# Two row gathers in place of one, four filler matmuls, and other cuts of two early loads

## The chip, the cores and the metric

The kernel runs on one core of a Trainium2 chip. Time is device microseconds (us) of one launch, the median of several runs. The core has a matrix engine (PE, whose loading of weights the profile lists as PEld), a vector engine (DVE), a scalar engine (ACT), a general engine (POOL) and a queue engine (SP). Loads and stores are issued from SP's, ACT's and POOL's queues and carried out by 16 DMA engines.

## The reference

```
xn = layernorm(x)                                   # x: 8 x 1 x 512
q  = (xn @ wq) as 32 heads of 128                   # wq: 512 x 4096
k, v = the last 2048 rows of 8192 of each of 8 heads, each shared by 4 query heads
p  = softmax(q . k * 128 ** -0.5)
s  = (p . v) @ wo                                   # wo: 4096 x 512
h  = sigmoid(xn @ w_gate) * (xn @ w_up)             # 512 x 1792 each
g  = silu(h @ w_down)                               # w_down: 1792 x 512
out = x + s * g                                     # 8 batches, bfloat16
```

Only the window of the caches is read: 2 MB of k and of v for each half of a batch's heads, 32 loads of 2 MB in all, beside some 13.6 MB of weights.

## The kernel before, in words

**The ring.** All large inputs pass through `ring`, nine slots of 16 KB in each of 128 partitions. A list `todo` holds the loads in order: w_gate (two loads of two rows of each partition), w_up, the last 1152 rows of w_down (`want_down`), the slot for the other 640 rows (`want_side`, cleared by DVE), wq (two slots), 17 drains of SP's queue, then k and v in turns with k three ahead, then wo in pieces of 16, 10, 4 and 2 rows. `pump` issues as long as slots are free; `free` gives slots back after the code that last reads them, so SP's queue waits at a load until PE has used up an older one. All but the gather go through SP's queue. The input x is loaded in five pieces from ACT's queue (L200).

**The gather.** The first 640 rows of w_down are 64 pieces of ten rows (10 KB). One indirect DMA on POOL's queue (L239) puts each into a partition of its own; `SEGS` (L139, L140) says into which: (start, count, step). The other 64 partitions are given an index beyond the bound and stay cleared. The index is made on the chip: `sel` (copies of columns of the identity, on POOL) times `ranks` on PE, turned into `which` on DVE. Which partition holds a piece decides which DMA engine writes it.

**Early work.** Layer norm of x (L256 to L267), its transposes (L278), w_gate (L323) and w_up (L339) matmuls, h, its 19 transposes (L358: nine for the direct rows, ten for the gathered), q (L387), a `spot` matmul that spreads the gathered part of h to the partitions in use (L398), 19 matmuls with w_down (L403), the transposes of q.

**The batch loop** (L675). For each of eight batches: transposes of k on PE (L484), copied by DVE (L489), scores (L502), maximum and exponentials (L515, L522), transposes of p (L591), and the products with v (L612) two batches behind. After the loop the last batches are finished: scores, `row_max`, `values`, `combine`, `normalise`, `turn`. Between these stand fillers, `keep(n)`: n matmuls of 480 columns into `idle_ps`, which nobody reads (L720). The product with wo (L372, `fin_ps`, 128 matmuls in two halves of 64), two DVE operations and two stores end the kernel.

Of the kernel before, what the change touches and what calls it, by code (L numbers as in the profile page):

```python
# [10 lines left out]
def kernel(  # L11
# [13 lines left out]
    nc = tc.nc  # L25
# [90 lines left out]
    def want_rows(name, w, per, r0, r1, steps):  # L116
        n = -(-(r1 - r0) * w.shape[1] // (CT * Dh))

        def f(k):
            t, where = room(k, n, r1 - r0, w.shape[1])  # L120
            a = r0
            for step in steps:
                q0.dma_start(
                    out=t[:, a - r0 : a - r0 + step, :].rearrange("p r n -> p (r n)"),
                    in_=w.rearrange("(p r) n -> p r n", r=per)[
                        :, a : a + step, :
                    ].rearrange("p r n -> p (r n)"),
                )
                a += step
            rows_of[(name, r0)] = (t, where)  # L130
            for r in range(r0, r1):
                weights[(name, r)] = t[:, r - r0, :]

        todo.append((n, f))

    MT = 9
    SF = 10
    NSEL = 64
    SEGS = [(0, 15, 1), (16, 3, 1), (28, 18, 1), (48, 2, 1)]  # L139
    SEGS += [(60, 8, 1), (68, 6, 4), (92, 8, 1), (124, 4, 1)]  # L140
    m0 = NSEL * SF
    assert sum(n for _, n, _ in SEGS) == NSEL and m0 + MT * P == F
    side = {}

    def want_side(w):
# [35 lines left out]

    RT = 32
    Z = 32
    want_rows("wg_sb", B_w_gate, KT, 0, KT, (2, 2))
    want_rows("wu_sb", B_w_up, KT, 0, KT, (KT,))
    want_down(B_w_down)
    want_side(B_w_down)
    want_rows("wq_sb", A_wq, KT, 0, KT, (KT,))
    todo.append((0, lambda k: [q0.drain() for _ in range(17)]))
    order = [(b, i) for b in range(B) for i in range(NQ)]  # L190
    AHEAD = 3
    for n in range(len(order) + AHEAD):
# [4 lines left out]
    want_rows("wo_sb", A_wo, RT, 0, RT, (16, 10, 4, 2))  # L197

    x_bf = work.tile([B, D], bf16, name="x_bf")
    for r, z in ((0, 2), (2, 4), (4, 6), (6, 7), (7, 8)):  # L200
        q1.dma_start(out=x_bf[r:z], in_=A_x.flatten_outer_dims()[r:z])

    eps_t = work.tile([B, 1], f32, name="eps_t")
# [4 lines left out]
    make_identity(nc, ident_f[:])  # L208
    pump()

    sel = consts.tile([NSEL, P], bf16, name="sel")
    nc.gpsimd.memzero(sel[:])
    at = 0
    for p, n, step in SEGS:
        nc.gpsimd.tensor_copy(
            out=sel[:, p : p + (n - 1) * step + 1 : step],
            in_=ident[:NSEL, at : at + n],
        )
        at += n
    ranks = consts.tile([NSEL, 1], bf16, name="ranks")  # L220
    nc.gpsimd.iota(
        ranks[:],
        pattern=[[0, 1]],
        base=P,
        channel_multiplier=-1,
        allow_small_or_imprecise_dtypes=True,
    )
    rank_ps = ps_m.tile([P, 1], f32, name="rank_ps", tag="m")
    nc.tensor.matmul(rank_ps[:], lhsT=sel[:], rhs=ranks[:], start=True, stop=True)
    which = consts.tile([P, 1], mybir.dt.uint32, name="which")  # L230
    nc.vector.tensor_scalar(
        out=which[:],
        in0=rank_ps[:],
        scalar1=-1.0,
        scalar2=float(P),
        op0=ALU.mult,
        op1=ALU.add,
    )
    nc.gpsimd.indirect_dma_start(  # L239
        out=side["t"].rearrange("p t n -> p (t n)"),  # L240
        out_offset=None,
        in_=B_w_down[:m0, :].rearrange("(p t) n -> p (t n)", t=SF),
        in_offset=bass.IndirectOffsetOnAxis(ap=which[:, :1], axis=0),
        bounds_check=NSEL - 1,
        oob_is_err=False,
    )

    perm = consts.tile([P, P], bf16, name="perm")
    nc.gpsimd.tensor_copy(
# [102 lines left out]
    free(rows_of[("wu_sb", 0)])  # L352
    hT_ps = ps_m.tile([P, MT + SF, B], bf16, name="hT_ps", tag="m")
    cuts = [h_bf[:B, m0:F].rearrange("b (p t) -> b t p", t=MT)[:, t] for t in range(MT)]
    cuts += [h_bf[:B, :m0].rearrange("b (p t) -> b t p", t=SF)[:, t] for t in range(SF)]
    rows = [P] * MT + [NSEL] * SF
    for t, x in enumerate(cuts):
        nc.tensor.transpose(  # L358
            out=hT_ps[: rows[t], t, :], in_=x, identity=ident[:B, :B]
        )  # L360
    nc.vector.tensor_copy(out=hT_sb[:, :MT, :B], in_=hT_ps[:, :MT])
    hc_sb = work.tile([NSEL, SF, B], bf16, name="hc_sb")
    nc.scalar.copy(out=hc_sb[:], in_=hT_ps[:NSEL, MT:])

    NG = NB // 2
    ZO = Z * NG
# [28 lines left out]
                )  # L395
    free(rows_of[("wq_sb", 0)])
    spot_ps = ps_t.tile([P, SF, B], f32, name="spot_ps", tag="t")
    nc.tensor.matmul(spot_ps[:], lhsT=sel[:], rhs=hc_sb[:], start=True, stop=True)  # L398
    nc.scalar.copy(out=hT_sb[:, MT:, :B], in_=spot_ps[:])
    d_ps = ps_s.tile([P, D], f32, name="d_ps", tag="s")  # L400
    for t in range(MT + SF):
# [93 lines left out]
    def scores(b, u):  # L495
        i, j = u // NJ, u % NJ
        if u == 0:
            s_ps[b] = ps_s.tile([P, CU * PG], f32, name="s_ps", tag="s")
        t = kT.pop((b, u))
        o = M0 - rep * u  # L500
        for l in range(G):
            nc.tensor.matmul(  # L502
                s_ps[b][NR * l : NR * (l + 1), :],
                lhsT=qm_sb[:, b, i * G + l, o : o + Z],
                rhs=t[:, :, PG * l : PG * (l + 1)],
                start=(u == 0),
                stop=(u == NU - 1),
                tile_position=(0, NR * l),
                skip_group_check=True,
            )  # L510


    def row_max(b):
        st[b] = small.tile([P, 1], f32, name="st")
        nc.vector.tensor_reduce(  # L515
            out=st[b][:], in_=s_ps[b][:], axis=AX.X, op=ALU.max, negate=True
        )
        sums = small.tile([P, 1], f32, name="sums")
        s = s_ps.pop(b)
        for l in range(G):  # L520
            rows = slice(NR * l, NR * (l + 1))
            nc.scalar.activation(  # L522
                out=p_buf[b % 2][rows, :, l, :],
                in_=s[rows, :].rearrange("k (c p) -> k p c", p=PG),
                func=AF.Exp,
                bias=st[b][rows, :],
                accum_out=sums[rows, :],
            )
        fac[b] = sums
# [56 lines left out]
    def p_transposes(b, h):  # L586
        if h == 0:
            pT[b] = ppool.tile([P, CU, P], bf16, name="pT_sb")
        pT_ps = ps_t.tile([P, CH, P], bf16, name="pT_ps", tag="t")
        for c in range(CH):  # L590
            nc.tensor.transpose(  # L591
                out=pT_ps[:, c, :],
                in_=p_buf[b % 2][:, :, :, h * CH + c].rearrange("k p l -> k (p l)"),
                identity=turn_rows[:],
            )
        nc.vector.tensor_copy(out=pT[b][:, h * CH : (h + 1) * CH, :], in_=pT_ps[:])  # L596
# [27 lines left out]
    def values(b, c):  # L624
        for i in range(NQ):
            value(b, i, c)

    def combine(b):
        del pT[b]
        n = NJ if b < WIDE else 2  # L630
        o = small.tile([P, NJ, Dh], f32, name="o_sb")
        nc.scalar.activation(  # L632
            out=o[:, :n], in_=o_ps[:, :n], func=AF.Copy, scale=fac.pop(b)[:]
        )
        row[b] = o

    def normalise(b, oT_ps=oT_ps):
        o = row.pop(b)
        sel = sel_j if b < WIDE else sel_e
        n = NJ if b < WIDE else 2  # L640
        for e in range(n):
            nc.tensor.matmul(  # L642
                oT_ps,
                lhsT=o[:, e, :],
                rhs=sel[:, e],
                start=(e == 0),
                stop=(e == n - 1),
            )

        oB = small.tile([P, Hq, NDQ], bf16, name="oB")  # L650
        nc.vector.tensor_tensor(
            out=oB[:],
            in0=oT_ps.unsqueeze(2).to_broadcast([P, Hq, NDQ]),
            in1=band[:].unsqueeze(1).to_broadcast([P, Hq, NDQ]),
            op=ALU.mult,
        )
        row[b] = oB

    def turn(b, oP_ps=oP_ps):
        nc.tensor.matmul(  # L660
            oP_ps,
            lhsT=row.pop(b)[:].rearrange("p s q -> p (s q)"),
            rhs=pick[:],
            start=True,
            stop=True,
        )
        nc.vector.tensor_copy(out=oP_sb[:, :, 2 + 2 * b], in_=oP_ps)
# [3 lines left out]
    def values_some(b, u):  # L671
        for c in range(CV * u, CV * (u + 1)):
            values(b, c)
# [24 lines left out]
                f()  # L698

    last = B - 1  # L700
    scores(last, NU - 1)
    values_some(last - 2, NU - 1)
    combine(last - 2)
    row_max(last)
    values(last - 1, 0)
    values(last - 1, 1)
    normalise(last - 2)
    for c in range(2, CU):
        values(last - 1, c)
        if c == 5:  # L710
            turn(last - 2)
    combine(last - 1)
    stat_rows(last)
    p_transposes(last, 0)
    idle_ps = ps_s.tile([P, 512], f32, name="idle_ps", tag="s")
    idle_in = qm_sb[:, 0].rearrange("k h m -> k (h m)")

    def keep(n):
        for _ in range(n):
            nc.tensor.matmul(  # L720
                idle_ps[:, : Hkv * (M0 + Z)],
                lhsT=ident[:],
                rhs=idle_in,
                start=True,
                stop=True,
            )

    keep(2)
    for c in range(CU // 2):
        value(last, 0, c)  # L730
# [65 lines left out]
```

## Time and profile before

| | us |
|---|---|
| median of 3 runs (lowest to highest) | 198.5 (198.39 to 198.58) |
| the profiled execution, its own time | 198.86 |
| its span on the core | 197.1 |
| PE busy, share of the span | 163.4 (83%) |
| DVE | 125.7 (64%) |
| ACT | 40.8 (21%) |
| POOL | 9.1 (5%) |

The span is the time from the first to the last instruction of the core; the rest of the execution's time lies around it. Busy times of engines overlap. A row of a timeline gives start, busy time, engine, line, operation, output and inputs, and in brackets the idle time before it with what ended it. A row of a chain gives start, duration and what the end had to wait for. A row of stretches gives the stretch, its length, busy time of each engine (with instructions), the clock granted to PE as a share of its full speed, the share of the 16 DMA engines in use, and GB/s.

### The profile page before, as it was taken

The numbers are of one execution on the slowest core, as the hardware profiler recorded it, in microseconds if no ns is written. First come the engines' busy times: TensorE is split into PE (matmuls) and PEld (weight loads), VectorE is DVE, ScalarE is ACT, GpSimd is POOL, SyncE is SP. The second block draws the span as 40 slices with busy tenths as digits, with TensorE's granted clock in tenths as the row PEclk, the third lists the DMA queues.
The fourth block names the chain that finished last, engine by engine and source line by source line (L and its number), as shares of the span: only waits on it lengthen the run. The fifth ranks groups of instructions, "written<-read, shape, count | busy, mean of one in ns | idle before, by whom it ended". The sixth has DMA issues, their size and how long they took to land.

```text
span 197.1 us, 4818 instructions
## 1 busy us (share of the span) xinstructions
PE 163.4 (83%) x2114; PEld 106.8 (54%) x2114; DVE 125.7 (64%) x247; ACT 40.8 (21%) x95; POOL 9.1 (5%) x31
## 2 busy tenths in 40 slices
PE   0029859999699999799979987999799998878883
PEld 0013423876576575456646654665467566655652
DVE  4540401999799796679667966796549878935201
ACT  0053003001701501600160016001600070071000
POOL 7910000000000000000000000000000000000000
PEclk9999966999999999999999999999879999999999
DMA  6999999999999999999999999999999999999990
GB/s 203 438 440 463 416 406 426 436 436 432 424 429 429 422 426 422 439 432 432 426 432 434 426 426 421 429 436 426 419 442 439 426 431 422 426 429 429 420 401 16
DMA packets 6148, 81.32 MB, mean 413 GB/s; under 512 B 808, under 2 KB 816, under 8 KB 1328
## 3 DMA queue, kind: packets, MB, share of 16 engines
q1 hardware_dynamic: 5936, 80.35, 96.0%
q0 software_dynamic: 144, 0.66, 0.8%
q8 instruction: 16, 0.26, 0.5%
q14 instruction: 4, 0.03, 0.0%
q10 hardware_dynamic: 48, 0.01, 0.0%
HBM read 81.67 MB, written 0.01 MB: 414 GB/s over the span
## 4 chain that ended last, share of the span: by engine, by line
DMA 65%; PE 25%; DVE 5%; ACT 3%; issue 1%; SPq 0%; ACTq 0%
DMA ring<-in_A_k_cache_dram 29%; DMA ring<-in_A_v_cache_dram 13%; PE kT_ps L484 13%; DMA ring<-in_A_wq_dram 11%; DMA ring<-in_A_wo_dram 10%; PE s_ps L502 4%; PE o_ps L612 3%; DMA ring<-in_B_w_gate_dram 3%; DVE kT_sb L489 2%; PE q_ps L387 2%; ACT p_buf L522 2%; PE fin_ps L372 1%; PE d_ps L403 1%; DVE pT_sb L596 1%; ACT L522 1%
## 5 line engine op out<-in xcount | busy, mean ns | idle before, releaser
L489 DVE COPY kT_sb<-kT_ps 128x1024 bf16<-128x1024 bf16 x128 | 84.3, 684 | 26.0 <-PE kT_ps L484 21.2
L484 PE MATMUL kT_ps<-perm,ring 128*128 128x128 bf16 x1024 | 73.4, 221 | 2.0 <-DMA ring<-in_A_k_cache_dram 2.0
L484 PEld LDWEIGHTS <-ring 128*128 128x128 bf16 x1024 | 59.5, 99 | 24.6 <-issue 18.3
L612 PE MATMUL o_ps<-ring,pT_sb 128*32 128x256 bf16 (+1 forms) x352 | 36.6, 330 | 6.6 <-DMA ring<-in_A_v_cache_dram 5.6
L502 PE MATMUL s_ps<-kT_sb,qm_sb 128*32 128x512 bf16 x256 | 25.8, 393 | 1.3 <-DVE kT_sb L489 1.1
L522 ACT ACTIVATE p_buf<-s_ps,st 32x512 bf16<-32x512 f32 x32 | 21.7, 679 | 15.5 <-DVE st L515 15.1
L612 PEld LDWEIGHTS <-pT_sb 128*32 128x32 bf16 (+1 forms) x352 | 12.4, 102 | 19.4 <-issue 17.6
L632 ACT ACTIVATE o_sb<-o_ps,fac 128x512 f32<-128x512 f32 (+1 forms) x8 | 4.9, 608 | 60.5 <-PE o_ps L612 60.5
L596 DVE COPY pT_sb<-pT_ps 128x1024 bf16<-128x1024 bf16 x16 | 10.8, 676 | 1.8 <-PE pT_ps L591 1.8
L502 PEld LDWEIGHTS <-qm_sb 128*32 128x32 bf16 x256 | 7.0, 93 | 8.1 <-issue 1.5
L591 PE MATMUL pT_ps<-turn_rows,p_buf 128*128 128x128 bf16 x128 | 10.7, 227 | 0.0
L591 PEld LDWEIGHTS <-p_buf 128*128 128x128 bf16 x128 | 9.4, 148 | 0.2 <-issue 0.2
L278 PE MATMUL xnT_ps<-ident,xn_bf 8*128 8x8 bf16 x4 | 0.3, 174 | 9.9 <-DVE xn_bf L267 9.9
L549 ACT ACTIVATE w_row<-w 1x128 f32<-1x128 f32 x8 | 2.5, 308 | 28.6 <-DVE w L542 28.6
L346 DVE TENSOR_TENSOR h_bf<-sig,u_ps 8x448 bf16<-8x448 f32 x4 | 2.4, 608 | 6.6 <-PE u_ps L339 6.1
L422 DVE COPY qm_sb<-qT_ps 128x128 bf16<-128x128 bf16 x2 | 1.4, 876 | 8.1 <-PE qT_ps L417 8.1
L323 PE MATMUL g_ps<-ring,xnT_sb 128*8 128x448 bf16 x16 | 5.7, 541 | 0.3 <-DVE xnT_sb L285 0.3
L522 ACT ACTIVATION_READ_ACCUMULATOR p_buf<-s_ps,st 32x1 f32 x32 | 5.9, 184 | 0.0
L515 DVE TENSOR_REDUCE st<-s_ps 128x1 f32<-128x512 f32 x8 | 5.5, 682 | 0.5 <-PE s_ps L502 0.5
L278 PEld LDWEIGHTS <-xn_bf 8*128 8x128 bf16 x4 | 0.2, 114 | 10.0 <-DVE xn_bf L267 10.0
L387 PE MATMUL q_ps<-ring,xnT_sb 128*32 128x512 bf16 x32 | 3.6, 629 | 2.4 <-DMA ring<-in_A_wq_dram 2.4
L642 PE MATMUL m_ps<-ident_f,o_sb 128*128 128x32 f32 x40 | 5.2, 272 | 0.0
(97 smaller groups left out, 97.0 us busy)
## 6 DMA issues: line engine op xcount, KB each, us to landing
ring<-in_A_k_cache_dram SPq DMA_DIRECT2D x16, 2048.0 KB, 28.5
ring<-in_A_v_cache_dram SPq DMA_DIRECT2D x16, 2048.0 KB, 30.4
ring<-in_A_wq_dram SPq DMA_DIRECT2D x1, 4096.0 KB, 21.6
ring<-in_A_wo_dram SPq DMA_DIRECT2D x1, 2048.0 KB
ring<-in_B_w_gate_dram SPq DMA_DIRECT2D x2, 896.0 KB, 6.0
ring<-in_B_w_up_dram SPq DMA_DIRECT2D x1, 1792.0 KB, 13.1
ring<-in_A_wo_dram SPq DMA_DIRECT2D x1, 1280.0 KB
ring<-in_B_w_down_dram SPq DMA_DIRECT2D x1, 1152.0 KB
```

What stands on the lines that cost most here:

```text
L323: nc.tensor.matmul(g_ps[:], lhsT=xnT_sb[:, kt, :B], rhs=weights[("wg_sb", kt)][:, k * FC : (k + 1) * FC], start=(kt == 0), stop=(kt == KT ...
L387: nc.tensor.matmul(q_ps[e][Z * g : Z * (g + 1), :], lhsT=xnT_sb[:, kt, :], rhs=weights[("wq_sb", kt)][:, c0 : c0 + D], start=(kt == 0), st ...
L484: nc.tensor.transpose(out=kT_ps[:, c, :], in_=k_sb[:, j * CU + h * CH + c, :], identity=perm[:],)
L489: nc.vector.tensor_copy(out=kT[(b, u)][:, h * CH : (h + 1) * CH, :], in_=kT_ps[:])
L502: nc.tensor.matmul(s_ps[b][NR * l : NR * (l + 1), :], lhsT=qm_sb[:, b, i * G + l, o : o + Z], rhs=t[:, :, PG * l : PG * (l + 1)], start=(u ...
L515: nc.vector.tensor_reduce(out=st[b][:], in_=s_ps[b][:], axis=AX.X, op=ALU.max, negate=True)
L522: nc.scalar.activation(out=p_buf[b % 2][rows, :, l, :], in_=s[rows, :].rearrange("k (c p) -> k p c", p=PG), func=AF.Exp, bias=st[b][rows, ...
L591: nc.tensor.transpose(out=pT_ps[:, c, :], in_=p_buf[b % 2][:, :, :, h * CH + c].rearrange("k p l -> k (p l)"), identity=turn_rows[:],)
L596: nc.vector.tensor_copy(out=pT[b][:, h * CH : (h + 1) * CH, :], in_=pT_ps[:])
L612: nc.tensor.matmul(o_ps[r] if b < WIDE else o_ps[r, 0:2], lhsT=pT[b][:, c, r], rhs=x, start=(c == 0), stop=(c == CU - 1), tile_position=(0 ...
L632: nc.scalar.activation(out=o[:, :n], in_=o_ps[:, :n], func=AF.Copy, scale=fac.pop(b)[:])
L642: nc.tensor.matmul(oT_ps, lhsT=o[:, e, :], rhs=sel[:, e], start=(e == 0), stop=(e == n - 1),)
```

## The change

`SEGS` becomes `SPOTS`: two lists, one for 60 pieces of eight rows and one for 40 of four, again 640 rows. Each has its own `sel`, `ranks`, index (the `rank_ps` tile now comes from the pool `ps_t`) and indirect DMA into its own part of the side slot, which is 12 rows wide in place of ten. h has 21 transposes, two copies and two spot matmuls for it, and 21 matmuls with w_down. w_gate is one load of four rows of each partition, and there are 18 drains in place of 17. x comes in six loads, batches 4 and 5 singly. `idle_ps` and `keep` are defined earlier, and `keep(2)` stands ahead of the last batch's last scores and behind its `row_max`.

```diff
-    SF = 10
-    NSEL = 64
-    SEGS = [(0, 15, 1), (16, 3, 1), (28, 18, 1), (48, 2, 1)]
-    SEGS += [(60, 8, 1), (68, 6, 4), (92, 8, 1), (124, 4, 1)]
-    m0 = NSEL * SF
+    SPOTS = [
+        (8, 60, [(0, 20, 1), (28, 18, 1), (48, 2, 1), (60, 8, 1), (92, 8, 1), (124, 4, 1)]),
+        (4, 40, [(0, 5, 4), (28, 16, 1), (44, 9, 2), (64, 4, 1), (92, 5, 1), (124, 1, 1)]),
+    ]
+    SF = sum(r for r, _, _ in SPOTS)
+    NSEL = max(n for _, n, _ in SPOTS)
+    m0 = sum(r * n for r, n, _ in SPOTS)
...
-    want_rows("wg_sb", B_w_gate, KT, 0, KT, (2, 2))
+    want_rows("wg_sb", B_w_gate, KT, 0, KT, (KT,))
...
-    todo.append((0, lambda k: [q0.drain() for _ in range(17)]))
+    todo.append((0, lambda k: [q0.drain() for _ in range(18)]))
...
-    for r, z in ((0, 2), (2, 4), (4, 6), (6, 7), (7, 8)):
+    for r, z in ((0, 2), (2, 4), (4, 5), (5, 6), (6, 7), (7, 8)):
...
+    for (r, count, _), sel in zip(SPOTS, sels):
+        base = row0 // r
...
+        rank_ps = ps_t.tile([P, 1], f32, name="rank_ps", tag="t")
...
+            scalar2=float(P + base),
...
-    nc.gpsimd.indirect_dma_start(
-        out=side["t"].rearrange("p t n -> p (t n)"),
-        in_=B_w_down[:m0, :].rearrange("(p t) n -> p (t n)", t=SF),
...
-        bounds_check=NSEL - 1,
+    for r, which, row1 in spots_which:
+        nc.gpsimd.indirect_dma_start(
+            out=side["t"][:, t0 : t0 + r].rearrange("p t n -> p (t n)"),
...
+            in_=B_w_down[:row1, :].rearrange("(p t) n -> p (t n)", t=r),
+            in_offset=bass.IndirectOffsetOnAxis(ap=which[:, :1], axis=0),
+            bounds_check=row1 // r - 1,
...
-    nc.scalar.copy(out=hc_sb[:], in_=hT_ps[:NSEL, MT:])
+    for r, count, _ in SPOTS:
+        nc.scalar.copy(
+            out=hc_sb[:count, t0 : t0 + r], in_=hT_ps[:count, MT + t0 : MT + t0 + r]
+        )
...
-    nc.tensor.matmul(spot_ps[:], lhsT=sel[:], rhs=hc_sb[:], start=True, stop=True)
+    for (r, count, _), sel in zip(SPOTS, sels):
+        nc.tensor.matmul(
+            spot_ps[:, t0 : t0 + r],
+            lhsT=sel[:],
+            rhs=hc_sb[:count, t0 : t0 + r],
...
+    keep(2)
     scores(last, NU - 1)
     values_some(last - 2, NU - 1)
     combine(last - 2)
     row_max(last)
+    keep(2)
     values(last - 1, 0)
```

More of the change, by code (lines that the diff above doesn't have):

```diff
@@ L136 @@
     MT = 9
-    SF = 10
-    NSEL = 64
-    SEGS = [(0, 15, 1), (16, 3, 1), (28, 18, 1), (48, 2, 1)]
-    SEGS += [(60, 8, 1), (68, 6, 4), (92, 8, 1), (124, 4, 1)]
-    m0 = NSEL * SF
-    assert sum(n for _, n, _ in SEGS) == NSEL and m0 + MT * P == F
+    SPOTS = [
[5 more added lines that the diff above has]
+    m0 = sum(r * n for r, n, _ in SPOTS)
+    assert m0 + MT * P == F
     side = {}
@@ L209 @@
     pump()
[L211 to L217, printed above, removed]
-        )
[L219 to L239, printed above, removed]
-        out=side["t"].rearrange("p t n -> p (t n)"),
-        out_offset=None,
-        in_=B_w_down[:m0, :].rearrange("(p t) n -> p (t n)", t=SF),
-        in_offset=bass.IndirectOffsetOnAxis(ap=which[:, :1], axis=0),
-        bounds_check=NSEL - 1,
-        oob_is_err=False,
-    )
+    sels = []
@@ new lines @@
+    for _, count, segs in SPOTS:
+        sel = consts.tile([count, P], bf16, name=f"sel{count}")
+        nc.gpsimd.memzero(sel[:])
+        at = 0
+        for p, n, step in segs:
+            nc.gpsimd.tensor_copy(
+                out=sel[:, p : p + (n - 1) * step + 1 : step],
+                in_=ident[:count, at : at + n],
+            )
+            at += n
+        assert at == count
+        sels.append(sel)
+    row0 = 0
+    spots_which = []
+    for (r, count, _), sel in zip(SPOTS, sels):
+        base = row0 // r
+        ranks = consts.tile([count, 1], bf16, name=f"ranks{count}")
+        nc.gpsimd.iota(
+            ranks[:],
+            pattern=[[0, 1]],
+            base=P,
+            channel_multiplier=-1,
+            allow_small_or_imprecise_dtypes=True,
+        )
+        rank_ps = ps_t.tile([P, 1], f32, name="rank_ps", tag="t")
+        nc.tensor.matmul(rank_ps[:], lhsT=sel[:], rhs=ranks[:], start=True, stop=True)
+        which = consts.tile([P, 1], mybir.dt.uint32, name=f"which{count}")
+        nc.vector.tensor_scalar(
+            out=which[:],
+            in0=rank_ps[:],
+            scalar1=-1.0,
+            scalar2=float(P + base),
+            op0=ALU.mult,
+            op1=ALU.add,
+        )
+        row0 += r * count
+        spots_which.append((r, which, row0))
@@ L248 @@
+    t0 = 0
+    for r, which, row1 in spots_which:
+        nc.gpsimd.indirect_dma_start(
+            out=side["t"][:, t0 : t0 + r].rearrange("p t n -> p (t n)"),
+            out_offset=None,
+            in_=B_w_down[:row1, :].rearrange("(p t) n -> p (t n)", t=r),
+            in_offset=bass.IndirectOffsetOnAxis(ap=which[:, :1], axis=0),
+            bounds_check=row1 // r - 1,
+            oob_is_err=False,
+        )
+        t0 += r
     perm = consts.tile([P, P], bf16, name="perm")
@@ L354 @@
     cuts = [h_bf[:B, m0:F].rearrange("b (p t) -> b t p", t=MT)[:, t] for t in range(MT)]
-    cuts += [h_bf[:B, :m0].rearrange("b (p t) -> b t p", t=SF)[:, t] for t in range(SF)]
-    rows = [P] * MT + [NSEL] * SF
+    rows = [P] * MT
+    row0 = 0
+    for r, count, _ in SPOTS:
+        x = h_bf[:B, row0 : row0 + r * count].rearrange("b (p t) -> b t p", t=r)
+        cuts += [x[:, t] for t in range(r)]
+        rows += [count] * r
+        row0 += r * count
     for t, x in enumerate(cuts):
@@ L362 @@
     hc_sb = work.tile([NSEL, SF, B], bf16, name="hc_sb")
-    nc.scalar.copy(out=hc_sb[:], in_=hT_ps[:NSEL, MT:])
+    t0 = 0
+    for r, count, _ in SPOTS:
+        nc.scalar.copy(
+            out=hc_sb[:count, t0 : t0 + r], in_=hT_ps[:count, MT + t0 : MT + t0 + r]
+        )
+        t0 += r
     NG = NB // 2
@@ L397 @@
     spot_ps = ps_t.tile([P, SF, B], f32, name="spot_ps", tag="t")
-    nc.tensor.matmul(spot_ps[:], lhsT=sel[:], rhs=hc_sb[:], start=True, stop=True)
+    t0 = 0
+    for (r, count, _), sel in zip(SPOTS, sels):
[3 more added lines that the diff above has]
+            rhs=hc_sb[:count, t0 : t0 + r],
+            start=True,
+            stop=True,
+        )
+        t0 += r
     nc.scalar.copy(out=hT_sb[:, MT:, :B], in_=spot_ps[:])
@@ L700 @@
     last = B - 1
[L701 to L714, printed above, removed]
     idle_ps = ps_s.tile([P, 512], f32, name="idle_ps", tag="s")
@@ L726, in keep @@
             )
+    keep(2)
+    scores(last, NU - 1)
+    values_some(last - 2, NU - 1)
+    combine(last - 2)
+    row_max(last)
+    keep(2)
+    values(last - 1, 0)
+    values(last - 1, 1)
+    normalise(last - 2)
+    for c in range(2, CU):
+        values(last - 1, c)
+        if c == 5:
+            turn(last - 2)
+    combine(last - 1)
+    stat_rows(last)
+    p_transposes(last, 0)
     keep(2)
```

## The prediction

> **What bounds the kernel now.** I read the page first, then the stretches, then the end of the chain in order of time, then the trace's own records of single DMA packets.
>
> ```profile
> span 197.1 us, 4818 instructions
> ...
> DMA  6999999999999999999999999999999999999990
> GB/s 203 438 440 463 416 406 426 436 436 432 424 429 429 422 426 422 439 432 432 426 432 434 426 426 421 429 436 426 419 442 439 426 431 422 426 429 429 420 401 16
> ...
> DMA 65%; PE 25%; DVE 5%; ACT 3%; issue 1%; SPq 0%; ACTq 0%
> ```
>
> The DMA engines are full from the second slice to the last but one; 81.3 MB pass, and no edit changes how many bytes of input are read.
>
> ```profile
> core 0: us, PE busy (x) PEld busy (x) DVE busy (x) ACT busy (x) POOL busy (x), PEclk, DMA share, GB/s
> 34.70:75.00 40.30, 37.84 (x538) 27.53 (x534) 36.93 (x71) 8.46 (x21) 0.00 (x0) 1.00 1.01 429
> 136.00:171.00 35.00, 32.72 (x436) 22.03 (x433) 26.12 (x54) 8.16 (x20) 0.00 (x0) 0.95 1.01 431
> 184.00:194.00 10.00, 8.78 (x174) 6.31 (x169) 0.63 (x3) 0.47 (x1) 0.00 (x0) 1.00 0.81 338
> ```
>
> The share of DMA stays at 1.01 whether PE waits or not. SP's issues show why: the cache loads land 26.4 to 33.7 us after their issue. Set against the packet records, each load from wq on (the fifth) is issued at least 7.8 us before the first DMA engine could start on it. So PE, DVE and ACT may be some us late without a DMA engine running dry.
>
> ```profile
> 171.83 19.82 DMA ring<-in_A_wo_dram
> 191.65 0.04 issue
> 191.69 2.24 PE fin_ps L372 x64
> 193.93 0.02 issue
> 193.96 0.29 DVE prod L756
> ```
>
> The 64 matmuls from 191.69 are not one run: by their single starts PE stops at 192.77 and again from 193.31 to 193.52, for the last two pieces of wo. Only 8 matmuls (0.4 us) follow that. So the end is set by when the **slowest of 16 DMA engines** has written its last piece of wo.
>
> The packet records carry no engine number, but in the steady stretch every engine takes one 16 KB piece each 607.8 ns, so its phase identifies it, and each load leaves 16 completion marks. Followed from load to load, with pieces counted by L139/L140:
>
> ```
> pieces of the gather   engines   last mark of wo, us
> 8                      6         191.99 192.07 192.23 192.30 192.68 192.89
> 5                      2         191.39 192.42
> 1                      6         191.08 192.23 192.24 192.31 192.43 193.15
> 0                      2         191.86 191.95
> ```
>
> The counts follow if a DMA engine serves four neighbouring partitions and the four that lie 32 further on; right after the gather the marks stand in just such groups (six late by 8 x 385 ns, two by 5 x 385 ns). What levels them later are fetches of instructions: sixteen of 16 KB, each delaying one engine by 1.42 us, two for each engine of the last two rows (one comes after its engine was done); two of 8 KB on the 192.42 (0.84 us each), one on the 191.39 (0.59) and one on the 192.89 (0.56). The 193.15 was late from the start: its first gate packet took 1868 ns, the others 411 to 1551, and its mark of the second gate half is 0.83 us behind the median. The mean of the sixteen is 192.20; perfect balance would be worth 0.95 us.
>
> **The change, part by part.**
>
> *Gathers.* From the records: a 10 KB piece holds its engine 385 ns, 9 KB 347, 7 KB 272, 4 KB 156. An 8 KB piece lies halfway, 310. The new lists give the six engines 8 pieces of 8 KB and 5 of 4 KB, the two of five 6 and 3, the two of none 0 and 2, the six of one nothing. Per engine: 8 x 310 + 5 x 156 - 3080 = **+180 ns**; 6 x 310 + 3 x 156 - 1925 = **+403**; 2 x 156 = **+312**; **-385**. A partition that is left out costs a 4-byte packet (9 ns); of these there are 3, 4, 6 and 9 more, so +27, +36, +54, +81.
>
> *Gate by one load.* An engine's 16 pieces of 7 KB (272) become 8 of 14 KB (535 in the w_up load): 4280 - 4352 = **-72 ns** everywhere. Unknown is the start: the first half's marks come at 4.83 us on average, where 1.77 + 8 x 0.272 = 3.95 would be free of start-up, so 0.88 us is lost. Bounds: with half the packets, half of it is lost (-0.44), or the same time is lost and the bigger first packet adds its own 0.26. I take the same loss (0), since the bytes and rows touched first are the same. SP's one issue less (0.41) brings w_up and w_down forward; both are issued 4.6 and 8.3 us before their turn, so that is worth nothing. One drain more costs SP 52 ns ahead of the first k load, which has 15.6 us in hand.
>
> *Input by six loads.*
>
> ```profile
> 3.88 1.17 POOL L239 DMA_INDIRECT ring<-in_B_w_down_dram,which  x1 [0.70 <-DVE which L231]
> 7.36 2.50 DVE L256 CAST x_f<-x_bf 8x512 f32<-8x512 bf16 x1 [3.78 <-DMA x_bf<-in_A_x_dram]
> 13.81 5.67 PE L323 MATMUL g_ps<-ring,xnT_sb 128*8 128x448 bf16 x16 [0.27 <-DVE xnT_sb L285]
> 27.61 3.60 PE L387 MATMUL q_ps<-ring,xnT_sb 128*32 128x512 bf16 x32 [2.40 <-DMA ring<-in_A_wq_dram]
> ```
>
> The second x load's packet is served at 4.56, directly behind the first gate mark of its engine; the rest take turns with gate packets until 6.9. With 535 ns packets the first comes behind 8 x 535 (about 6.7), and the turns take twice as long, plus one more load with two turns: 6.7 + 2 x 2.3 + 1.1 = 12.4, so the cast starts 3 to 6 us later (the gather's pieces take turns too). It leaves POOL's memsets behind and may then be nearer the 0.53 us of the like operation at L267. Q, which had 2.40 us in hand for wq, is then 0 to 4 us late. Queued behind it are d, the q transposes and all of k's work, and SP's waits for freed ring slots: the fourth k load had 18 us in hand, later ones 16 to 28, wo 9.5. PE catches up as before, when it first waited for DMA at 75.1; with 13 us of waits for k and v (5.9 + 5.6 + 2.0 in the waits) from there to 171, a further 4 us are gone by about 110. Cost on the path 0; if the cover were gone, those 4 us. Moving one row's packet from one engine to another is 54 ns. The wq load waits for the second x load and had 7.8 us in hand.
>
> *Index work for two gathers.* POOL: four copies (1.08/8 each), a memset (0.14), an iota (0.13), a second indirect DMA (1.17): 2.0 us; behind it in POOL's queue stand perm and the memsets, last to end at 10.2 and first needed at 25.3 (hT_sb). DVE: the ring memset 2.19 x 12/10, and one index of 0.13. The gather landed at 15.5 and is first used after 31.3, so up to 3 us more is hidden. PE: ten matmuls (2 transposes, a rank, a spot, 2 for d, 4 fillers); the first six are 0.8 us, in the stretch just covered; ACT: one copy (0.22), one issue (0.27).
>
> *Fillers.*
>
> ```profile
> 138.40:141.80 3.40, 2.16 (x25) 1.73 (x24) 1.62 (x4) 3.03 (x8) 0.00 (x0) 0.99 1.05 443
> 141.80:145.20 3.40, 3.40 (x29) 1.96 (x27) 1.22 (x3) 0.06 (x1) 0.00 (x0) 0.50 0.98 419
> 172.48:175.89 3.41, 2.52 (x53) 1.72 (x56) 1.42 (x4) 2.37 (x6) 0.00 (x0) 1.00 1.01 428
> ```
>
> The clock was halved after a stretch with PE busy 2.16 of 3.40 and not after one with 2.52. Two fillers took 0.57; each new pair falls into a gap of about that size (0.58 for kT_sb at 172.7, 0.63 for o_sb at 174.0). Cost 0, bounded by 1.14, of which 0.8 us is hidden (fin's first half waited from 187.87, when oP_sb was done, to 188.7 for wo). Gain 0 here, since the clock was full to the end already.
>
> **The sum**, last marks with all terms (+0.14, +0.37, -0.38, +0.29): six engines to 192.82 and 193.03, two to 192.79, six to 192.77, two to 192.24. The last is now 193.03 in place of 193.15: **-0.12 us**. The profiled run is 198.86 (span 197.08 and 1.78 around it), so 198.74; it lies 0.36 above the median of 198.5, to which the same step gives **198.4**. The rebalancing is right in sign, but the 192.89 engine gets more bytes and takes over.
>
> **Rivals.**
>
> *Start-up halves with the packets* (faster). For: 256 packets become 128, and the long ones are the first of each engine. Against: address and bytes are the same. The last engine comes to 193.03 - 0.44 - 0.12 (its share of a narrower spread) = 192.47: 198.5 - 0.68 = 197.8; with half that, 198.15.
>
> *The late starter is among the six* (slower). The first packets' spread is 1.4 us. If the 0.83 falls on the 192.89 engine, its mark is 193.86, +0.71: 199.2. Decides once it is late by over 0.5. Against: runs lie within 0.19 us, so start-up seems to repeat. The Trainium skill (DMA: Bandwidth & Descriptors, Latency and other measured facts) says that DMA engines 7 and 15, which this list counts among the six, are usually slower, perhaps through the software gather's descriptor rings; in this trace all sixteen take 607.8 ns a piece, which speaks against it.
>
> *Late input and the clock* (slower). PE's first idle after catching up comes later, and with it the half clock moves from 141.8 into 172 to 188. One such stretch of 3.4 us costs PE 1.7; 0.8 is in hand before fin and 0.35 in its second half, leaving 0.55: 199.05; two leave 2.25: 200.75. It decides once PE is over 1.1 us late. Against: the fillers raise the weakest stretch, 2.52 of 3.41. The Trainium skill (TensorE: Matmul & The Clock Gate, Why this matters for your kernels) asks for no PE gap above about 3 us; by it no stretch here could lose the clock, but this trace lost it with no gap above 1.24 us.
>
> That the pieces do not reach the engines named is unlikely, since the present list did.
>
> **Chances.** Forecast 0.54 (198.1 to 198.85), start-up 0.30, late starter 0.08, clock 0.08. About 0.2% (0.4 us) is what a measurement of this kernel can tell from no change: faster 0.30, same 0.54, slower 0.16. Range 197.7 to 199.0, from the start-up rival's full gain to near the slower ones.
>
> **What would show it.** Six engines' marks up by 0.1 to 0.2 us and six down by 0.4; the last marks between 192.9 and 193.1; g_ps first at 17 to 20 us; DMA share 1.0 throughout; clock full from 172 on. Wrong if a DMA engine has a gap between pieces, or the last 8 matmuls don't wait for wo.

## The result, and the profile after

The changed kernel takes 198.98 us (median of 13 runs, 198.72 to 199.14) against 198.43 (13 runs, 198.32 to 198.62) for the kernel before: ratio 1.0024, 95% interval 1.0016 to 1.0031. It is slower by about 0.5 us. Ranges of single runs below leave out those that lie over 1 us above the others of their kernel.

The profiled run of the changed kernel took 199.11 us. Its page, in the lines that were shown of before, and the row of the granted clock:

```profile
span 197.2 us, 4851 instructions
...
PEclk9999966999999999999999999999999999999999
DMA  6999999999999999999999999999999999999990
GB/s 204 426 435 451 427 412 429 429 432 429 424 432 432 429 425 429 432 432 425 429 435 427 425 429 427 435 425 429 425 439 425 424 429 432 432 429 422 425 400 17
...
DMA 65%; PE 25%; DVE 5%; ACT 3%; issue 1%; SPq 0%; ACTq 0%
```

The same stretches of the changed kernel, and the stretch of 3.41 us that was the weakest for PE in the tail of before:

```profile
34.70:75.00 40.30, 37.64 (x530) 27.15 (x531) 36.93 (x71) 8.62 (x22) 0.00 (x0) 1.00 1.01 429
136.00:171.00 35.00, 31.41 (x437) 21.16 (x434) 26.20 (x52) 8.17 (x20) 0.00 (x0) 1.00 1.01 430
184.00:194.00 10.00, 8.83 (x174) 6.29 (x171) 0.88 (x3) 0.47 (x1) 0.00 (x0) 1.00 0.83 349
172.48:175.89 3.41, 3.22 (x49) 1.69 (x45) 1.56 (x3) 2.01 (x5) 0.00 (x0) 1.00 1.02 437
```

Still bound by its transfers, with the DMA share at 1.01, and PE at full clock from 33.4 us to the end. PE's weakest stretch in the tail, where the fillers stand, rose from 2.52 to 3.22 of 3.41 us, and nothing came of it. The early rows of the timeline and the end of the chain in order of time:

```profile
11.21 0.77 DVE L271 CAST x_f<-x_bf 8x512 f32<-8x512 bf16 x1 [6.83 <-DMA x_bf<-in_A_x_dram]
15.94 5.06 PE L338 MATMUL g_ps<-ring,xnT_sb 128*8 128x448 bf16 x16 [0.27 <-DVE xnT_sb L300]
28.26 3.60 PE L412 MATMUL q_ps<-ring,xnT_sb 128*32 128x512 bf16 x32 [1.62 <-DMA ring<-in_A_wq_dram]
```

```profile
172.20 19.57 DMA ring<-in_A_wo_dram
191.77 0.04 issue
191.81 2.26 PE fin_ps L397 x64
194.07 0.02 issue
194.09 0.29 DVE prod L792
```

x is cast 3.85 us later, q starts 0.65 us later and still waits for wq. At the end everything from the product with wo on lies 0.1 us later: the last mark of wo is at 193.33 us (193.15 in the profiled run of before). The difference came in at the start, as the experiments below show. In the first microseconds (a row: stretch, length, busy times of PE, PEld, DVE, ACT and POOL, clock, DMA share, GB/s), first the kernel before, then the changed one:

```profile
2.00:3.00 1.00, 0.00 (x0) 0.00 (x0) 1.00 (x1) 0.00 (x0) 1.00 (x8) 1.00 0.53 143
3.00:4.00 1.00, 0.16 (x1) 0.10 (x1) 0.58 (x2) 0.00 (x0) 0.29 (x3) 1.00 0.91 358
4.00:5.00 1.00, 0.00 (x0) 0.00 (x0) 0.00 (x0) 0.00 (x0) 1.00 (x1) 1.00 1.07 447
```

```profile
2.00:3.00 1.00, 0.00 (x0) 0.10 (x1) 1.00 (x1) 0.00 (x0) 0.94 (x8) 1.00 0.62 143
3.00:4.00 1.00, 0.06 (x1) 0.06 (x1) 1.00 (x1) 0.00 (x0) 0.97 (x8) 1.00 0.60 258
4.00:5.00 1.00, 0.18 (x2) 0.05 (x1) 0.30 (x3) 0.00 (x0) 0.41 (x1) 1.00 1.00 430
```

Between 3 and 4 us the changed kernel moves 258 GB/s in place of 358. Three of its DMA engines need 2.24 to 2.39 us for their first packet of 14 KB, and their marks behind w_gate (the 4-byte packet with which an engine ends its part of a load) come at 7.84, 7.97 and 7.97 us; the other thirteen lie at 6.62 to 7.45. The sum over all engines does not decide: the kernel before with w_gate by one load (below) moves 1062 KB in its first 5 us by such rows, no fewer than the 1050 KB of before, and is as slow as the changed kernel (1005 KB). What counts is how late the latest engines are.

### The profile page after: what moved, and what is told of

It reads as the page before. It is cut to its first block, busy times and chain, and to the rows that moved or that the text cites. A ratio compares the mean times of both kernels' runs of the same rounds, so it can differ in the third digit from the quotient of the medians.

```text
span 197.2 us, 4851 instructions
## 1 busy us (share of the span) xinstructions
PE 162.6 (82%) x2124; PEld 106.2 (54%) x2124; DVE 124.6 (63%) x248; ACT 40.9 (21%) x96; POOL 10.7 (5%) x38
## 4 chain that ended last, share of the span: by engine, by line
DMA 65%; PE 25%; DVE 5%; ACT 3%; issue 1%; SPq 0%; ACTq 0%
DMA ring<-in_A_k_cache_dram 29%; DMA ring<-in_A_v_cache_dram 13%; PE kT_ps L518 13%; DMA ring<-in_A_wq_dram 10%; DMA ring<-in_A_wo_dram 10%; DMA ring<-in_B_w_gate_dram 4%; PE s_ps L536 4%; PE o_ps L646 3%; DVE kT_sb L523 2%; PE q_ps L412 2%; ACT p_buf L556 2%; PE fin_ps L397 1%; PE d_ps L437 1%; DVE pT_sb L630 1%; ACT L556 1%
## 5 line engine op out<-in xcount | busy, mean ns | idle before, releaser
L518 PE MATMUL kT_ps<-perm,ring 128*128 128x128 bf16 x1024 | 72.6, 220 | 1.8 <-DMA ring<-in_A_k_cache_dram 1.8
L518 PEld LDWEIGHTS <-ring 128*128 128x128 bf16 x1024 | 58.8, 98 | 24.0 <-issue 17.4
L646 PE MATMUL o_ps<-ring,pT_sb 128*32 128x256 bf16 (+1 forms) x352 | 36.1, 327 | 6.9 <-DMA ring<-in_A_v_cache_dram 6.4
L338 PE MATMUL g_ps<-ring,xnT_sb 128*8 128x448 bf16 x16 | 5.1, 495 | 0.3 <-DVE xnT_sb L300 0.3
L271 DVE CAST x_f<-x_bf 8x512 f32<-8x512 bf16 x1 | 0.8, 774 | 6.8 <-DMA x_bf<-in_A_x_dram 6.8
```

The lines of the kernel that those rows point to most:

```text
L338: nc.tensor.matmul(g_ps[:], lhsT=xnT_sb[:, kt, :B], rhs=weights[("wg_sb", kt)][:, k * FC : (k + 1) * FC], start=(kt == 0), stop=(kt == KT ...
L518: nc.tensor.transpose(out=kT_ps[:, c, :], in_=k_sb[:, j * CU + h * CH + c, :], identity=perm[:],)
L646: nc.tensor.matmul(o_ps[r] if b < WIDE else o_ps[r, 0:2], lhsT=pT[b][:, c, r], rhs=x, start=(c == 0), stop=(c == CU - 1), tile_position=(0 ...
```

## The experiments

Theory S says that the start costs the time (the single load of w_gate), theory G that the new shares of the gathers do. The last mark of wo is read from the packet records as in the prediction; it belongs to the profiled execution, which is not always the median one. Medians in us, with the kernel before measured beside them:

```
kernel                        median  before  ratio   95% interval      last mark
gate by one load              199.09  198.51  1.0021  0.9999 to 1.0043  193.27
two gathers                   198.68  198.51  1.0016  0.9984 to 1.0048  192.96
six x loads                   198.54  198.51  0.9997  0.9975 to 1.0018  192.78
four fillers                  198.53  198.51  0.9996  0.9975 to 1.0018  192.82
gate 1 + 3 rows               198.51  198.53  1.0002  0.9993 to 1.0011  192.75
gate 3 + 1 rows               198.80  198.53  1.0014  1.0005 to 1.0023  193.24
gate 1 + 1 + 2 rows           198.55  198.53  1.0003  0.9994 to 1.0012  192.78
changed kernel, gate 2 + 2    198.71  198.53  1.0010  1.0001 to 1.0019  192.93
pieces by counts (one run)    200.33  198.75                            194.67
pieces levelled               198.15  198.40  0.9985  0.9951 to 1.0020  192.40
the same, gate 1 + 3          198.38  198.40  0.9998  0.9990 to 1.0007  192.46
pieces levelled, again        198.32  198.53  0.9997  0.9982 to 1.0012  192.68
```

In all of them, and in both kernels, the profiled execution's own time is its last mark plus 5.64 to 5.82 us.

**Each part alone.** Gate by one load:

```diff
-    want_rows("wg_sb", B_w_gate, KT, 0, KT, (2, 2))
+    want_rows("wg_sb", B_w_gate, KT, 0, KT, (KT,))
-    todo.append((0, lambda k: [q0.drain() for _ in range(17)]))
+    todo.append((0, lambda k: [q0.drain() for _ in range(18)]))
```

> The kernel before with w_gate by one load (and 18 drains, which keeps SP's instruction count), nothing else. Theory S (the start): the whole loss comes from here, since the first packet of each DMA engine doubles and no packet can finish before it: the gate's last marks move from a mean of 6.98 to 7.16 us or later, and the time is up by 0.3 to 0.55 us. Theory G (the gathers' shares): the time is down by 0.07 or unchanged.

Up by 0.58 us. The interval just touches 1, for it takes in one run of before at 200.72 us; the other single runs do not overlap: 198.91 to 199.22 against 198.27 to 198.80. The end of its chain shows PE waiting for the last piece of wo, with 8 matmuls behind it:

```profile
191.81 1.84 PE fin_ps L372 x56
193.65 0.00 issue
193.65 0.41 PE fin_ps L372 x8
```

Theory S holds on where and how much, but not on the mean of the gate marks: it is 7.04, as in the profiled run of before (6.98 and 6.91 in the filler and x variants). What moved is the latest ones: 7.82, 7.90 and 7.92, against 7.45 and 7.41 for the latest in the filler and x variants. (In the profiled run of before the latest stood at 7.78, then 7.52.)

The two gathers (`SPOTS` and all that belongs to it, the rest as before):

> The kernel before with the two gathers alone (60 pieces of 8 rows, 40 of 4), gate by two loads, input by five, 17 drains, no new fillers. Theory S: within 0.1 us of before (my sum for the gathers without the start: -0.05 against the profiled run of before). Theory G: the engines that were last already get 0.18 to 0.4 us more, so the time is up by 0.3 to 0.5 us, and the gate's marks stay at a mean of 6.98.

Up by 0.17 at the median, inside its interval: between the theories. Its last mark belongs to the engine with DVE's two instruction fetches, 192.96, where that engine ends at 192.60 and 192.61 in the x and filler variants.

x in six loads, `(4, 6)` split into `(4, 5), (5, 6)`, and the fillers, `keep(2)` ahead of the last scores and behind `row_max(last)`:

> The kernel before with x in six loads alone. Both theories: within 0.1 us of before; the cast of x starts under 1.5 us later. A third theory X (a late input costs time further on) wants 0.2 us or more here.

> The kernel before with the four fillers alone. Theories S and G: within 0.1 us of before, since PE waits for wo at 187.9 to 188.7 in either case. If the fillers cost, fin's first half starts later than the landing of wo's first piece and the time is up by more than 0.2.

0.03 and 0.02 us: neither counts. The cast of x starts at 8.05 in place of 7.36.

**The size of the first packet.** The edits are `(1, 3)`, `(3, 1)` and `(1, 1, 2)` for `(2, 2)`, the last with 16 drains.

> The kernel before with w_gate in loads of one and three rows of each partition (first packets of 3.5 KB in place of 7), the same number of loads and drains. Theory S (what the first packet of a DMA engine moves can't overlap with anything): first packets half as long in service, the gate's last marks 0.1 us earlier in the mean than with (2, 2), time down by 0.1 to 0.3 us. Theory L (the number and order of loads matters, not the packet): within 0.1 us of before.

> The kernel before with w_gate in loads of three and one rows (first packets of 10.5 KB), the same number of loads and drains. Theory S: half of what the single load cost, up by 0.2 to 0.4 us. Theory L: within 0.1 us of before.

> The kernel before with w_gate in three loads of one, one and two rows, and 16 drains. Theory S: as with (1, 3), or a little better (marks early), time down by 0.1 to 0.4 us, unless the third load's 0.4 us of SP's issue lets a DMA engine run dry, which would show as gaps between gate packets before 4 us. Theory L: a third load moves the time by as much as the second did, down by 0.5.

Theory L falls: with the same two loads in the other order the time differs by 0.29 us. Upwards the size tells step by step:

```
first packet  latest first packet ends  latest gate mark  median
3.5 KB        2.75                      7.39              198.51
7 KB          3.42, 3.38                7.45, 7.41        198.53 (kernel before)
10.5 KB       3.97                      7.87              198.80
14 KB         4.19                      7.92              199.09
```

(The row of 7 KB shows the filler and x variants.) The late marks follow from the end of the first packet: behind it these engines run without a gap, 7 more packets of 0.53 us from 4.19 to 7.92, or 15 of 0.27 us from 3.42 to 7.45. So the first packet ends some 0.8 us later, the rest is 0.3 us shorter, and 0.5 us are left. Theory S's other half is a miss: below 7 KB nothing is won. With 3.5 KB the first packets end earlier, but the marks' mean was 7.16 in this trace. With the same two loads in the levelled kernel below it was 6.86, so one trace does not show that the engines lose the gain again, and why the time stays was not tried.

**The changed kernel with the gate as before:**

> The changed kernel with w_gate by two loads again (and 17 drains): two gathers, six x loads and four fillers are left. If the gate and the gathers are the only parts that count: as the gathers alone, 0.1 to 0.25 us above before. If x or the fillers cost something beside the gathers: 0.3 or more. If the parts help each other: at or below before.

0.18 above before: the cost of the gathers and no more. Its last mark is again that of the engine with DVE's fetches (192.93). So the gate is worth 0.27 us in the changed kernel by the two medians, 0.37 if each is set against the before measured beside it, and 0.58 in the kernel before. The parts do not add up (0.58 + 0.17 against 0.55 measured) because the end takes the latest of sixteen: in the changed kernel the gathers bring the engine with DVE's fetches to 193.00, and the start brings two others to 193.02 and, one of the six with most pieces, 193.33.

**Where a piece lies.** To test the shares by themselves, the 64 pieces of before were laid so that the eight engines with PE's fetches had 0 to 7 pieces, the six 2 to 8, the other two 1 and 4:

```diff
-    SEGS = [(0, 15, 1), (16, 3, 1), (28, 18, 1), (48, 2, 1)]
-    SEGS += [(60, 8, 1), (68, 6, 4), (92, 8, 1), (124, 4, 1)]
+    SEGS = [(0, 13, 1), (16, 4, 1), (24, 1, 1), (28, 11, 1), (40, 2, 1), (60, 1, 1), (64, 3, 1),
+            (68, 2, 1), (72, 3, 1), (76, 18, 1), (112, 1, 1), (116, 2, 1), (120, 3, 1)]
```

> The kernel before with its 64 ten-row pieces put elsewhere, so that each DMA engine has a count of its own within its group (from 0 to 8; the heaviest among the eight that also carry PE's instruction fetches has 7, the next 6). Theory G (a piece costs its engine 385 ns and the slowest engine alone sets the end): an engine with two of PE's fetches and no piece ends at about 191.9 us, so one with 7 pieces ends at 194.6 and the time is 200.3 us, or 199.9 if the one with 7 is the one whose second fetch comes after its end. If the pieces' place did not matter (the shares level out), the time would stay within 0.2 us of before.

A last mark of 194.67 and 200.33 us for 194.6 and 200.3. Nothing levels the engines but what they carry. The counts also name them: PE's fetches go round over the engines that begin at partitions 76, 80, 84, 88, 20 and 24 (these two may be the other way round), 68 and 72; DVE's fetches fall on the one from 12, SP's on the one from 16, ACT's on the one from 4. Two of the three late starters of the changed kernel are the seventh and eighth of the round, from 68 and 72; the third is one of the six. It is most likely the one from 64, their neighbour: in this run the three latest marks of w_gate are those of 68, 72 (7.26 each) and 64 (7.18), and in both runs of the levelled kernel below the latest (7.25 and 7.45) is that of 64. So the same engines tend to start late with 7 KB too, only by less.

Worked out from these marks, a placement that takes pieces from the engines that end last:

```diff
+    SEGS = [(0, 20, 1), (20, 2, 4), (28, 11, 1), (40, 4, 1), (48, 4, 1)]
+    SEGS += [(60, 8, 1), (72, 4, 4), (92, 7, 1), (124, 4, 1)]
```

> The kernel before (one gather of ten-row pieces, gate by two loads) with the pieces moved off the engines that end last: the engine with DVE's two instruction fetches 4 in place of 5, the one with ACT's fetch 7 in place of 8, the one with SP's fetch 8 in place of 5, two of PE's eight engines 0 in place of 1, the two with none 1 each, one of the six 7. Theory G: worked out from the marks of the run with counts of their own, the last marks lie at 192.0 to 192.45, which with the start's scatter of 0.3 us makes the last 192.4 to 192.7 in place of 192.8: time down by 0.1 to 0.4 us, beating both kernels. If the scatter of the start is larger than the levelling, within 0.1 us of before.

> The same placement with w_gate in loads of one and three rows, whose gate marks lay closer together (latest 7.39 us) though later in the mean (7.16). If the spread of the start decides: as fast as the levelled kernel or faster. If the mean does: 0.1 to 0.25 us behind it.

> The levelled kernel once more, for an interval of its own. If the gain is real: last mark at 192.3 to 192.6 us, 0.15 to 0.4 us below before. If the first measurement was luck with the start: within 0.1 us of before.

The end of the levelled kernel's chain in its first run (last mark 192.40):

```profile
190.97 2.25 PE fin_ps L372 x64
193.21 0.02 issue
193.24 0.29 DVE prod L756
```

The last operations start 0.85 us earlier than in the changed kernel. The medians are 0.25 and 0.21 us below the kernel before measured beside them, and below the changed kernel; but against the kernel before both intervals hold 1, so the gain there is likely, not shown. With `(1, 3)` it is 0.02, and the median lies 0.23 behind the levelled kernel's, as the reading by the mean has it. But the ranges overlap (198.11 to 198.64 against 198.09 to 198.49), and the profiled run, at 198.11 the fastest of its eleven, had its marks early (mean 6.86, latest 7.09), so this run does not tell the two readings apart.

## Why the prediction was wrong

It forecast 198.4 and no difference that can be told; measured were 198.98, near the upper end of its range, and 0.24%, clear of the interval.

- *The bound and the mechanism* were right: the slowest DMA engine's last piece of wo sets the end. Last mark plus a constant gives the time of thirteen further traces, and the placement by counts hit its forecast within 0.1 us.
- *The gate by one load* is the step that failed: "I take the same loss (0)", with 0.26 as the upper bound. The bound was one for a mean, and by the mean it nearly held (the changed kernel's marks have 7.16, those of before 7.04). But the end depends on the latest engines, and there the bigger packets cost about 0.5: latest first packet 4.19 us in place of 3.4, latest mark 7.92 in place of 7.4. Alone it measured +0.58; the saving of 72 ns that the packet times promised is not to be seen beside it. In the table of the sum the row that failed is that of the six with most pieces, forecast to end by 193.03: the late one of them ended at 193.33, with its gate mark at 7.97. Why these engines start late, and why a bigger first packet makes it worse there, stays open. (The first half's marks of before average 4.87 by the records, not 4.83, which changes nothing.)
- *The base of the sum.* The profiled run of before stood 0.36 us above the median, and I carried this over as if it were the same for both. It was the late starter: its 193.15 is not met again in the four other traces with the gate as two halves and the pieces of before or the two gathers (192.78 to 192.96). Most of my -0.12 was the relief of that one engine. Against 192.8 the same table, whose last was 193.03 (193.10 without the gate's 0.07), would have said +0.2 to +0.3, and the gathers alone then measured +0.17 and +0.18. That is in part luck, for another engine came out last than the table named.
- *The shares of the gathers.* The new pieces took what was forecast (309 and 159 ns for 310 and 156). The term for the two engines of five pieces was +0.44 without the gate's part; the one with DVE's fetches moved by 0.32 to 0.40. That this one and not the 192.89 engine would come out last was missed: in the changed kernel they end at 193.00 and 192.63.
- *Late input, clock, fillers, index work.* No cost, as forecast. The cast came 3.85 us later (forecast 3 to 6), g at 15.94, earlier than the 17 to 20 forecast, q 0.65 late, the smallest time in hand behind wq stayed 9.5 us at wo, and the clock was full from 33.4 on. The rival of late input falls. But that PE's busy time decides on the clock, as the part on fillers reads it, is not shown: in before the stretch from 97.39 to 100.80 us had PE busy for 2.16 us too, and the clock stayed full behind it.
- *The rivals.* "Start-up halves with the packets" had the sign wrong. "The late starter is among the six" comes closest: it priced 199.2, and the last mark is that of a late starter of the six. I gave it 0.08 because I took start-up to repeat with one engine late, the one of 193.15. It does repeat, but on three: with 14 KB packets two engines of the round and one of the six were late in both traces, and in before the second latest mark of w_gate (7.52) was already that of one of the six. The Trainium skill's remark that DMA engines 7 and 15 are usually slower (DMA: Bandwidth & Descriptors, Latency and other measured facts) is not borne out: with no piece they would have ended at 188.7 and 189.2 us in the run by counts, amid the 188.7 to 189.3 of those of their group that carry no fetch.

## What to carry to other kernels

Where the transfers bind and nothing waits inside, follow each DMA engine to its last piece and price an edit on the latest engine, not on the mean; what an engine loses in its first microseconds, or carries beside the others, it still lacks at the end. Begin the stream with small packets per engine (here up to 7 KB) even if the load could be one. Before working a sum out from one profiled run, see how far that run lies from the median, and if it does, look for what is odd in it.

## What the hardware showed that was not expected

Instruction fetches ride on the same DMA engines as the data: 16 blocks of 16 KB for PE, going round over eight of the sixteen engines, delay their engine by 1.42 us each, and 8 KB blocks for DVE, ACT and SP by 0.55 to 0.84; that is as much as 1.4 to 3.7 of the gather's 10 KB pieces (385 ns). The records do not name whose instructions a block holds. The large ones are put down to PE because its matmuls and weight loads are 4228 of the 4818 instructions; how the four small ones divide among DVE, ACT and SP is inferred and not shown, but the sums need only which DMA engine carries them. The first packet of an engine takes 0.3 to 1.9 us at 7 KB and 0.5 to 2.4 at 14 KB, where later ones take 0.27 and 0.54.
